# Alternating the order of head-group pairs, so that the last pair's streamed weights serve two steps

## The chip, the cores and the metric

The kernel runs on one core of one Trainium2 chip. The metric is the device time of one execution in microseconds (us), the median of several runs. The profile is one execution taken by the hardware profiler; its span is a little shorter than the device time. Engines are named as in the profile: PE is TensorE's matmul, PEld its weight load, DVE VectorE, ACT ScalarE, POOL GpSimd, SP SyncE, whose queue issues nearly all DMAs here.

## The reference

Four layers are applied to `x` (2048 tokens of 640): A, B, A, B, each with a layer norm before it and a residual around it. The two A layers have the same weights, and so have the two B layers.

```python
def _A_ref(x, mem0, Wq, Wk, Wv, Wo, seg_len):      # 32 heads of 192, 8 memory rows, segments of 32
    mem = mem0
    for s in range(n_seg):                         # 64 segments, one after the other
        h = jnp.concatenate([mem, x[:, s*seg_len:(s+1)*seg_len, :]], axis=1)   # 40 rows
        q, k, v = (jnp.einsum('btd,dhe->bhte', h, W) for W in (Wq, Wk, Wv))
        p = softmax(where(mask, einsum('bhqe,bhke->bhqk', q, k) * scale, -1e9))
        o = jnp.einsum('bhqk,bhke->bhqe', p, v)
        o = jnp.einsum('bhte,hed->btd', o, Wo)
        mem = o[:, :M, :]                          # the memory of the next segment
        outs.append(o[:, M:, :])

def _B_ref(x, w1, w2, w3, w4):                     # a mixer with shifts over tokens, and an MLP
    h = _gelu(_layernorm(x) @ w1)
    x1 = x + shifted(h) @ w2
    return x1 + _gelu(_layernorm(x1) @ w3) @ w4
```

The attention layer is a recurrence: a segment needs the memory rows that the segment before it made. With 40 rows a segment, each weight tile that is loaded into the array serves only 40 columns of moving data. Wq, Wk, Wv and Wo have 7.9 MB each[...].

## The kernel before

**Steps and lanes.** The work is cut into 69 steps (`T_A`). Lane 0 is the first A layer, lane 1 the second A layer, five segments behind (`LAG`). In step `t`, lane 0 handles segment `t` and lane 1 segment `t - 5`, with the same weights. In steps 0 to 4 only lane 0 runs, in steps 64 to 68 only lane 1; the 59 steps between have both. Matmuls of a two-lane step have 80 moving columns, those of a one-lane step `W = max(ONE, 40)`, which is 40. The B layers are computed in chunks of two segments for both lanes at once (`chunk`, `chunk_end`), spread over the attention steps; the last chunk runs alone at the end.

**Inside a step.** The 32 heads are 8 groups of 4, and two groups make a pair. For each of the 4 pairs, `proj_pair` makes k, q and v of both groups (L553: 90 matmuls a group). Then `attend` runs per group: scores (L618), mask and minimum (L629), exponential (L636), row sums and division (L640 to L642), transpose (L651) and its copy (L656), product with v (L665), the copy `oT` out of PSUM (L681), and the output projection (L692: 30 matmuls a group), which adds up in `psy` over the whole step. v itself is made in columns, copied (L583), transposed (L591) and copied into `V` by ACT and DVE in two halves (L602, L600). At the end of a step, L710 copies the new memory rows out of `psy` into `hT`, the moving operand of the next step's projections.

**Weights.** All of Wo stays on the chip, and so does a part of Wq, Wk and Wv: of the five contraction tiles of each kind, `STREAM` says how many are streamed (k 3, q 3, v 2), and `MORE` makes one more tile of k resident for pair 1. The others are loaded in every step, by `load_pair`, into a ring of 8 slots (`RING_A`, tile `wst`, 384 KB a load, L461). A pair has 8 streamed tiles (pair 1 has 7). The B weights stream through a second ring of three slots (`wstB`).

**The order of the work.** Nothing is scheduled by hand. Every operation is given to `Plan.add` with an engine, a cost, a due time and the buffers it reads and writes; `Plan.place` then simulates the engines and places, at each point, the operation that can start first (within 0.12 us on PE, the one with the earliest due time). The program is emitted in this order, and each engine runs its own list in order. PSUM tiles and ring slots are given out as they come free in this simulation. Loads form two queues in order of due time: `wa` for attention weights, `wb` for B weights, both issued by SP. A load is also held back until the simulated DMA is at most `DMA_AHEAD` behind (1 us; `DMA_AHEAD_ONE`, 2 us, where one lane runs). Where this holds a load back, it is made to wait for the last PE operation planned to be over by then. The simulated DMA moves 350 GB/s (`DMA_RATE`), and 385 in the first step (`DMA_START`).

Of the kernel before, what the change touches and what calls it, by code (L numbers as in the profile page):

```python
# [20 lines left out]
LAG = 5  # L21
# [3 lines left out]
MORE = {("k", 1): 1}  # L25
RING_B = 3
STEP = 48.0
Y_POOL = "A"
PSUM_POOLS = {"A": 6, "B": 2}
OT_BUFS = 8  # L30
KT_BUFS = 2
VT_BUFS = 2
HALVES = ()
ONE = 40
WARM = (2, 4, 2, 1, 1, 1, 1, 6, 1, 1, 2, 1, 1)
LAT = 0.12
PE_LAT = 0.3
DMA_RATE = 350.0e3
DMA_ISSUE = 0.37
DMA_FIRST = 0.8  # L40
DMA_LAST = 3.2
B_MARGIN = 0.6
LEAD_A = 0.0
LEAD_B = 0.0
DMA_AHEAD = 1.0
DMA_AHEAD_ONE = 2.0
DMA_START = 385.0e3
NSTEPS = 64
LAST_PACE = 0.55

# [30 lines left out]
class Plan:  # L81
# [48 lines left out]
    def place(self):  # L130
        in_queue = {}
        head = {}
        for q, lst in self.queues.items():
            lst.sort(key=lambda o: (o.due, o.i))
            for k, o in enumerate(lst):
                in_queue[o.i] = (q, k)
            head[q] = 0
        engines = sorted({o.e for o in self.ops})
        cand = {e: [] for e in engines}
        free = dict.fromkeys(engines, 0.0)  # L140
        waiting = {}

        def offer(o):
            if o.i in in_queue:
                q, k = in_queue[o.i]
                if k != head[q]:
                    waiting[o.i] = o
                    return
            cand[o.e].append(o)

        for o in self.ops:
            if o.n == 0:
                offer(o)
        left = len(self.ops)
        srv = 0.0
        out = []

        def est(o, t):
            s = max(t, o.ready)
            need = {}  # L160
            for b in o.slots:
                if b.slot is None:
                    need[b.cls] = need.get(b.cls, 0) + 1
            for c, n in need.items():
                fs = self.free_slots[c]
                if len(fs) < n:
                    return None
                s = max(s, fs[n - 1][0])
            if o.e == "SP":
                s0 = s  # L170
                s = max(s, srv - ahead(o))
                o.paced = s > s0 + 1e-9
            return s

        def ahead(o):
            if o.due < STEP:
                return 1.0e9
            return DMA_AHEAD_ONE if o.due < LAG * STEP or o.due >= NSTEPS * STEP else DMA_AHEAD

        while left:  # L180
            best = None
            for e in engines:
                t = free[e]
                lst = cand[e]
                if not lst:
                    continue
                vals = []
                m = None
                for o in lst:
                    s = est(o, t)  # L190
                    if s is not None:
                        vals.append((s, o))
                        if m is None or s < m:
                            m = s
                if m is None:
                    continue
                if best is not None and m >= best[0]:
                    continue
                lim = m + (0.12 if e == "PE" else 0.05)
                s, o = min((so for so in vals if so[0] <= lim), key=lambda so: (so[1].due, so[1].i))  # L200
                if best is None or s < best[0]:
                    best = (s, o)
            assert best is not None, "no operation can be placed"
            s, o = best
            e = o.e
            for b in o.slots:
                if b.slot is None:
                    b.slot = self.free_slots[b.cls].pop(0)[1]
            o.start = s
            o.end = s + o.d  # L210
            free[e] = o.end
            done = o.end
            if o.dma:
                srv = max(s + DMA_FIRST, srv) + o.dma / (DMA_START if o.due < STEP else DMA_RATE)
                done = srv + DMA_LAST + o.margin
            cand[e].remove(o)
            out.append(o)
            left -= 1
            for b in o.slots:
                b.left -= 1  # L220
                b.free_at = max(b.free_at, done + LAT)
                if b.left == 0:
                    heapq.heappush(self.free_slots[b.cls], (b.free_at, b.slot))
                    self.free_slots[b.cls].sort()
            for x in o.succ:
                if o.dma:
                    at = done
                elif x.e == e:
                    at = o.end
                else:  # L230
                    at = o.end + (PE_LAT if e == "PE" else LAT)
                if at > x.ready:
                    x.ready = at
                x.n -= 1
                if x.n == 0:
                    offer(x)
            if o.i in in_queue:
                q, k = in_queue[o.i]
                head[q] = k + 1
                lst = self.queues[q]  # L240
                if k + 1 < len(lst) and lst[k + 1].i in waiting:
                    x = waiting.pop(lst[k + 1].i)
                    cand[x.e].append(x)
        return out
# [3 lines left out]
def kernel(  # L248
# [17 lines left out]
    P = 128  # L266
    _, S, Dm = A_x.shape
# [8 lines left out]
    NG = H // HG  # L276
    GW = HG * Dh
    GC = GW // P
    GWH = GW // 2
    PW = 2 * GW  # L280
    NPAIR = NG // 2
# [17 lines left out]
    Wo_v = A_Wo.rearrange("h e d -> (h e) d").rearrange("(g c p) d -> p g c d", c=GC, p=P)  # L299
# [150 lines left out]
    def load_pair(kind, pr, due, now):  # L450

        nres = KC - STREAM[kind] + MORE.get((kind, pr), 0)
        cols = slice(PW * pr, PW * (pr + 1))
        rb, rt = res_tile((kind, pr), [P, nres, PW], w_src[kind][:, 0:nres, cols], due)
        slots = []
        for j, kc in enumerate(range(nres, KC)):
            b = Slotted("ra", None)
            b.make = lambda b=b: wring.tile([P, SLOT], bf16, name="wst", tag=f"ra{b.slot}")

            def fn(op, b=b, kc=kc):  # L460
                nc.sync.dma_start(out=T(b)[:, 0:PW], in_=w_src[kind][:, kc, cols])  # L461
            add("SP", DMA_ISSUE, due - now + 0.01 * j, fn, w=(b,), dma=2 * P * PW, queue="wa")
            slots.append(b)

        def view(kc, c0, c1):
            if kc < nres:
                return rt[:, kc, c0:c1]
            return T(slots[kc - nres])[:, c0:c1]
        return (rb, *slots), view
# [35 lines left out]
        return b, view  # L505


    def lanes(t):
        r = []
        if t < NSEG:  # L510
            r.append(0)
        if 0 <= t - LAG < NSEG:
            r.append(1)
        return r
# [4 lines left out]
    def attention_step(t):  # L519
# [9 lines left out]
        base = t * STEP  # L529
# [4 lines left out]
        first_wo = [True]  # L534
        nxt = lanes(t + 1)

        def proj_pair(pr):
            s0 = base + sl * 2 * pr
            for kind, at in (("k", 0.0), ("q", 0.2), ("v", 0.5)):
                wbs, wv = load_pair(kind, pr, s0 + at * 2 * sl, LEAD_A)  # L540
                for j in range(2):
                    g = 2 * pr + j
                    G = t * NG + g
                    due = s0 + (at + 0.1 * j) * 2 * sl
                    pq = ps("A", [P, GC, NS], f32, "ps" + kind)

# [56 lines left out]
                            add("DVE" if hf else "ACT", 0.35 if hf else act_us(GWH), due, fe, r=(pvt,),  # L603
                                w=(B("V", G % VT_BUFS, hf),))

        def attend(g):
            G = t * NG + g
            s0 = base + sl * g
            q, k_, V_ = qT, kT[G % KT_BUFS], Vt[G % VT_BUFS]
            pss = ps("A", [P, HG * NS], f32, "pss")  # L610
            hi = s0 + 0.5 * sl
# [56 lines left out]
            o_ = oT[G % OT_BUFS]  # L668

            oks = [B("oT", G % OT_BUFS, hf) for hf in range(2)]  # L670
            if g in HALVES:
                for hf in range(2):
                    def f7(op, hf=hf):
                        if hf:
                            nc.scalar.copy(out=o_[:, 3:6, off:off + N], in_=T(pso)[:, 3:6, 0:N])
                        else:
                            nc.vector.tensor_copy(out=o_[:, 0:3, off:off + N], in_=T(pso)[:, 0:3, 0:N])
                    add("ACT" if hf else "DVE", (act_us if hf else dve_us)(3 * N), hi - 4, f7, r=(pso,), w=(oks[hf],))
            else:
                def f7(op):  # L680
                    nc.vector.tensor_copy(out=o_[:, :, off:off + N], in_=T(pso)[:, :, 0:N])  # L681
                add("DVE", dve_us(GC * N), hi - 4, f7, r=(pso,), w=oks)
            due = base + STEP - 1 + 0.02 * g if g >= NG - OT_BUFS + 1 else s0 + 2.0 * sl
            wb, wo = res_tile(("o", g), [P, GC, Dm], Wo_v[:, g], base + STEP - 2 + 0.02 * g)
            for hf in range(2):
                def f8(op, hf=hf):
                    o = T(psy)
# [5 lines left out]
                                             rhs=o_[:, cc, 0:W], start=st, stop=True, skip_group_check=True)  # L693
                add("PE", mm_us(W, k=3 * KC), due, f8, r=(wb, oks[hf]), a=(psy,))

        for pr in range(NPAIR):
            proj_pair(pr)
            attend(2 * pr)
            attend(2 * pr + 1)

        due = base + STEP - 5
        hn = hT[(t + 1) % 4]
# [605 lines left out]
```

## Time and profile before

| | |
|---|---|
| time, median of 3 runs (lowest to highest) | 3512.29 us (3511.93 to 3518.08) |
| span of the profiled execution | 3501.2 us |
| granted clock of TensorE, mean | 0.980 |
| DMA in all | 1075.25 MB, 307 GB/s |
| loads of `wst` in the attention layers: q, k, v | 828, 759, 552 |
| loads of `wstB` | 495 of 320 KB, 132 of 160 KB |
| median time from the issue to the landing of a `wst` load | 5.2 to 5.4 us |
| copy of `oT` out of PSUM, two lanes (L681) | 472 of 654 ns |
| the same, one lane | 80 of 404 ns |

The profile comes in several views. The page gives busy time and the span in 40 slices: a digit is tenths of the slice, and PEclk the clock granted to TensorE in tenths of full speed. A second view cuts the span at given times. A third is the chain of waits, followed back from the last instruction. A fourth lists which engine waited for which: the waiting line, what it waited for, then microseconds in total, number of times and the longest. "Issue" there is idle time for which the profile shows no wait. The mean duration of a matmul in the lists contains its passage through the array, which overlaps with the next one; what a stream of matmuls costs is the distance of their starts.

### The profile page before, as it was taken

The numbers are of one execution on the slowest core, as the hardware profiler recorded it, in microseconds if no ns is written. First come the engines' busy times: TensorE is split into PE (matmuls) and PEld (weight loads), VectorE is DVE, ScalarE is ACT, GpSimd is POOL, SyncE is SP. The second block draws the span as 40 slices with busy tenths as digits, with TensorE's granted clock in tenths as the row PEclk, the third lists the DMA queues.
The fourth block names the chain that finished last, engine by engine and source line by source line (L and its number), as shares of the span: only waits on it lengthen the run. The fifth ranks groups of instructions, "written<-read, shape, count | busy, mean of one in ns | idle before, by whom it ended". The sixth has DMA issues, their size and how long they took to land.

```text
span 3501.2 us, 187978 instructions
## 1 busy us (share of the span) xinstructions
PE 3319.2 (95%) x84571; PEld 3225.6 (92%) x84573; DVE 2466.0 (70%) x7360; ACT 1519.5 (43%) x3573; POOL 235.3 (7%) x489
## 2 busy tenths in 40 slices
PE   5889999999999999999999999999999999999887
PEld 5889999999999999999999999999999999999776
DVE  2556777777777777777677777777777777777554
ACT  1334444444444444444444444444444444444333
POOL 1000000000000000000000000000000000000000
PEclk6999999999999999999999999999999999999999
DMA  9999898889888988898889888988898889888996
GB/s 375 319 312 314 301 322 294 297 299 322 306 309 299 323 304 306 305 320 304 294 307 323 302 297 297 323 306 308 308 325 302 293 304 315 301 305 298 316 307 222
DMA packets 497886, 1075.25 MB, mean 307 GB/s; under 512 B 49424, under 2 KB 217055, under 8 KB 497080
## 3 DMA queue, kind: packets, MB, share of 16 engines
q1 hardware_dynamic: 489784, 1050.15, 86.5%
q8 instruction: 661, 10.83, 1.2%
q0 software_dynamic: 7136, 13.00, 1.1%
q14 instruction: 145, 1.19, 0.1%
q10 hardware_dynamic: 160, 0.08, 0.0%
HBM read 1057.79 MB, written 5.24 MB: 304 GB/s over the span
## 4 chain that ended last, share of the span: by engine, by line
PE 90%; DMA 4%; issue 3%; DVE 2%; ACT 1%; SPq 0%; POOL 0%; POOLq 0%; DVEq 0%; ACTq 0%
PE psy L692 16%; PE psq L553 16%; PE psk L553 16%; PE psv L553 15%; PE pvt L591 5%; PE pso L665 4%; PE pss L618 4%; PE psh L1102 3%; PE y L1147 3%; PE pst L651 2%; DMA wst<-in_A_Wk_dram 2%; PE psh L980 1%; PE hs L1039 1%; DMA wst<-in_A_Wq_dram 1%; PE psv L753 1%
## 5 line engine op out<-in xcount | busy, mean ns | idle before, releaser
L553 PEld LDWEIGHTS <-wst 128*128 128x128 bf16 x25668 | 1030.7, 100 | 35.8 <-issue 23.4
L692 PE MATMUL psy<-oT,wo 128*128 128x80 bf16 (+1 forms) x16560 | 689.1, 199 | 34.7 <-issue 20.1
L692 PEld LDWEIGHTS <-wo 128*128 128x128 bf16 x16560 | 625.5, 100 | 44.2 <-issue 32.0
L563 ACT CAST qT<-psq 128x480 bf16<-128x480 f32 (+1 forms) x552 | 292.1, 529 | 630.5 <-PE psq L553 628.9
L553 PE MATMUL psq<-hT,wst 128*128 128x80 bf16 (+1 forms) x9936 | 468.2, 199 | 7.2 <-DMA wst<-in_A_Wq_dram 3.6
L681 DVE CAST oT<-pso 128x480 bf16<-128x480 f32 (+1 forms) x552 | 341.2, 618 | 160.8 <-PE pso L665 155.5
L553 PE MATMUL psv<-hT,wv 128*128 128x80 bf16 (+1 forms) x9936 | 433.9, 199 | 16.4 <-issue 12.9
L553 PE MATMUL psk<-hT,wst 128*128 128x80 bf16 (+1 forms) x9108 | 427.6, 199 | 10.0 <-issue 7.6
L656 ACT COPY PT<-pst 80x320 bf16<-80x320 bf16 (+1 forms) x552 | 221.6, 402 | 437.4 <-PE pst L651 429.8
L553 PEld LDWEIGHTS <-wv 128*128 128x128 bf16 x9936 | 386.1, 99 | 23.4 <-issue 14.7
L602 ACT COPY V<-pvt 80x384 bf16<-80x384 bf16 x552 | 261.5, 474 | 329.8 <-PE pvt L591 301.1
L553 PE MATMUL psk<-hT,wk 128*128 128x80 bf16 (+1 forms) x7452 | 349.2, 199 | 22.8 <-issue 11.5
L629 DVE CUSTOM_DVE_ANT_1 pss<-pss,mask 80x320 f32<-80x320 f32 (+2 forms) x552 | 253.8, 474 | 143.0 <-PE pss L618 136.7
L577 DVE CAST kT<-psk 64x160 bf16<-64x160 f32 (+1 forms) x1104 | 336.6, 305 | 9.8
L636 ACT ACTIVATE Pm<-pss,sm 80x320 bf16<-80x320 f32 (+2 forms) x552 | 279.3, 506 | 136.0 <-DVE sm L629 135.8
L583 ACT CAST vF<-psv 128x480 bf16<-128x480 f32 (+1 forms) x552 | 289.6, 525 | 103.9 <-PE psv L553 97.9
L553 PE MATMUL psv<-hT,wst 128*128 128x80 bf16 (+1 forms) x6624 | 322.6, 199 | 11.6 <-issue 10.5
L553 PE MATMUL psq<-hT,wq 128*128 128x80 bf16 (+1 forms) x6624 | 319.7, 199 | 7.7 <-issue 3.7
L553 PEld LDWEIGHTS <-wk 128*128 128x128 bf16 x7452 | 299.0, 100 | 29.5 <-issue 29.0
L600 DVE COPY V<-pvt 80x384 bf16<-80x384 bf16 x552 | 188.5, 350 | 174.6 <-PE pvt L591 102.4
L571 DVE CAST kT<-psk 128x320 bf16<-128x320 f32 (+1 forms) x552 | 254.5, 461 | 71.5 <-PE psk L553 65.1
L591 PE MATMUL pvt<-ident,vF 128*128 128x128 bf16 x3312 | 282.3, 222 | 10.1 <-issue 7.3
(139 smaller groups left out, 4354.3 us busy)
## 6 DMA issues: line engine op xcount, KB each, us to landing
wst<-in_A_Wq_dram SPq DMA_DIRECT2D x828, 384.0 KB, 5.3
wst<-in_A_Wk_dram SPq DMA_DIRECT2D x759, 384.0 KB, 5.2
wst<-in_A_Wv_dram SPq DMA_DIRECT2D x552, 384.0 KB, 5.4
wstB<-in_B_w_dram SPq DMA_DIRECT2D x495, 320.0 KB, 4.9
wstB<-in_B_w_dram SPq DMA_DIRECT2D x132, 160.0 KB, 4.6
wo<-in_A_Wo_dram SPq DMA_DIRECT2D x8, 960.0 KB, 12.5
wv<-in_A_Wv_dram SPq DMA_DIRECT2D x4, 1152.0 KB, 11.7
wq<-in_A_Wq_dram SPq DMA_DIRECT2D x4, 768.0 KB, 11.7
```

The costliest lines, as they stand in the source:

```text
L553: nc.tensor.matmul(out=o[:, cc, 0:W], lhsT=wv(kc, GW * j + cc * P, GW * j + (cc + 1) * P), rhs=h[:, kc, cw:cw + W], start=(kc == 0 and cc ...
L563: nc.scalar.copy(out=q[:, :, c0:c0 + N], in_=T(pq)[:, :, off:off + N])
L571: nc.vector.tensor_copy(out=k4[:, :, 0::3, c0:c0 + N], in_=p4[:, :, 0::2, off:off + N])
L577: nc.vector.tensor_copy(out=k4[r0:r1, :, jj, c0:c0 + N], in_=p4[r0:r1, :, 1, off:off + N])
L583: nc.scalar.copy(out=vF[:, :, c0:c0 + N], in_=T(pq)[:, :, off:off + N])
L591: nc.tensor.transpose(out=o[0:w_, c * P:(c + 1) * P], in_=vFw[:, c * NS:c * NS + w_], identity=ident[:, :])
L602: nc.scalar.copy(out=dst, in_=src)
L629: nc.vector.tensor_tensor_reduce(out=o, in0=o, in1=maskt.unsqueeze(1).to_broadcast([NR, HG, N]), scale=-scale, scalar=3.0e38, op0=ALU.add, ...
L636: nc.scalar.activation(out=Pb[0:NR, :, c0:c0 + N], in_=o, func=ACT.Exp, bias=sm_[0:NR, 0:1], scale=-1.0)
L656: nc.scalar.copy(out=Pt[:, :, 0:N], in_=T(pst)[0:NS, :, c0:c0 + N])
L681: nc.vector.tensor_copy(out=o_[:, :, off:off + N], in_=T(pso)[:, :, 0:N])
L692: nc.tensor.matmul(out=o[:, m, cw:cw + W], lhsT=wo[:, cc, m * P:(m + 1) * P], rhs=o_[:, cc, 0:W], start=st, stop=True, skip_group_check=True)
```

## The change

The four pairs of head groups are gone through from 0 to 3 in even steps and from 3 to 0 in odd ones. The pair that ends a step then begins the next one, and its streamed tiles can stay in the ring: they are loaded once for two steps. The buffers of k, V and `oT` now go by the position in the step, and the weights by the true number of the group.

With it come three settings. `HALVES` makes the copy `oT` two copies in every group, one of DVE and one of ACT. `ONE` widens the matmuls of one-lane steps from 40 to 56 columns; the additional 16 columns aren't used, and what they are for is to keep TensorE more active. And the plan of the one-lane steps expects 400 GB/s (`RATE_ONE`) and holds loads to 1 us ahead in place of 2.

```diff
+KEEP = True
-HALVES = ()
-ONE = 40
+HALVES = tuple(range(8))
+ONE = 56
-DMA_AHEAD_ONE = 2.0
+DMA_AHEAD_ONE = 1.0
+RATE_ONE = 400.0e3
...
-                srv = max(s + DMA_FIRST, srv) + o.dma / (DMA_START if o.due < STEP else DMA_RATE)
+                srv = max(s + DMA_FIRST, srv) + o.dma / (DMA_START if o.due < STEP else RATE_ONE if alone(o) else DMA_RATE)
...
+    kept = {}
...
-        def proj_pair(pr):
-            s0 = base + sl * 2 * pr
+        def proj_pair(i_, pr):
+            s0 = base + sl * 2 * i_
             for kind, at in (("k", 0.0), ("q", 0.2), ("v", 0.5)):
-                wbs, wv = load_pair(kind, pr, s0 + at * 2 * sl, LEAD_A)
+                if i_ == 0 and t > 0 and KEEP:
+                    wbs, wv = kept[kind]
+                else:
+                    wbs, wv = load_pair(kind, pr, s0 + at * 2 * sl, LEAD_A)
+                if i_ == NPAIR - 1:
+                    kept[kind] = wbs, wv
...
-            if g in HALVES:
+            if p_ in HALVES:
...
-        for pr in range(NPAIR):
-            proj_pair(pr)
-            attend(2 * pr)
-            attend(2 * pr + 1)
+        for i_ in range(NPAIR):
+            pr = NPAIR - 1 - i_ if t % 2 and KEEP else i_
+            proj_pair(i_, pr)
+            attend(2 * i_, 2 * pr)
+            attend(2 * i_ + 1, 2 * pr + 1)
```

In the same way `attend` takes the position `p_` beside the group `g`: due times and buffers go by `p_`, and only the tile of Wo goes by `g`.

More of the change, by code (lines that the diff above doesn't have):

```diff
@@ L177, in ahead, with alone @@
                 return 1.0e9
-            return DMA_AHEAD_ONE if o.due < LAG * STEP or o.due >= NSTEPS * STEP else DMA_AHEAD
+            return DMA_AHEAD_ONE if alone(o) else DMA_AHEAD
+        def alone(o):
+            return o.due < LAG * STEP or o.due >= NSTEPS * STEP
         while left:
@@ L535, in attention_step @@
         nxt = lanes(t + 1)
-        def proj_pair(pr):
-            s0 = base + sl * 2 * pr
+        def proj_pair(i_, pr):
+            s0 = base + sl * 2 * i_
             for kind, at in (("k", 0.0), ("q", 0.2), ("v", 0.5)):
-                wbs, wv = load_pair(kind, pr, s0 + at * 2 * sl, LEAD_A)
+                if i_ == 0 and t > 0 and KEEP:
[4 more added lines that the diff above has]
+                    kept[kind] = wbs, wv
                 for j in range(2):
-                    g = 2 * pr + j
-                    G = t * NG + g
+                    G = t * NG + 2 * i_ + j
                     due = s0 + (at + 0.1 * j) * 2 * sl
@@ L604, in proj_pair, with attend @@
                                 w=(B("V", G % VT_BUFS, hf),))
-        def attend(g):
-            G = t * NG + g
-            s0 = base + sl * g
+        def attend(p_, g):
+            G = t * NG + p_
+            s0 = base + sl * p_
             q, k_, V_ = qT, kT[G % KT_BUFS], Vt[G % VT_BUFS]
@@ L682, in attend @@
                 add("DVE", dve_us(GC * N), hi - 4, f7, r=(pso,), w=oks)
-            due = base + STEP - 1 + 0.02 * g if g >= NG - OT_BUFS + 1 else s0 + 2.0 * sl
-            wb, wo = res_tile(("o", g), [P, GC, Dm], Wo_v[:, g], base + STEP - 2 + 0.02 * g)
+            due = base + STEP - 1 + 0.02 * p_ if p_ >= NG - OT_BUFS + 1 else s0 + 2.0 * sl
+            wb, wo = res_tile(("o", g), [P, GC, Dm], Wo_v[:, g], base + STEP - 2 + 0.02 * p_)
             for hf in range(2):
```

## The prediction

> **What bounds the kernel now.** I read the page first, then busy time by step, then the chain of waits in two short windows, then who waits for whom in the stages with two lanes and with one.
>
> The page: TensorE is busy almost all the time, the weights stream on one queue, and TensorE's clock is below full only near the two ends.
>
> ```profile
> PE 3319.2 (95%) x84571; PEld 3225.6 (92%) x84573; DVE 2466.0 (70%) x7360; ACT 1519.5 (43%) x3573; POOL 235.3 (7%) x489
> ...
> PEclk6999999999999999999999999999999999999999
> DMA  9999898889888988898889888988898889888996
> ...
> q1 hardware_dynamic: 489784, 1050.15, 86.5%
> ...
> q8 instruction: 661, 10.83, 1.2%
> ```
>
> Busy time cut at the 68 `hT` copies of L710, which end the steps (us; then busy time and count by engine, clock, DMA share, GB/s):
>
> ```profile
> 88.10:133.20 45.10, 37.51 (x1152) 35.47 (x1152) 20.41 (x81) 13.81 (x41) 0.00 (x0) 0.88 0.93 321
> ...
> 278.30:3232.40 2954.10, 2887.82 (x72353) 2824.77 (x72350) 2180.42 (x6300) 1342.49 (x3064) 202.06 (x411) 1.00 0.89 307
> ...
> 3280.00:3328.90 48.90, 41.92 (x1206) 39.44 (x1204) 24.89 (x94) 16.84 (x50) 4.53 (x8) 0.87 0.93 312
> ...
> 3427.80:3501.00 73.20, 54.57 (x1308) 45.68 (x1309) 35.47 (x122) 21.60 (x62) 1.86 (x4) 0.92 0.60 204
> ```
>
> The 59 two-lane steps take 2954.1/59 = 50.1 us each. The one-lane steps are hardly shorter (190.2/4 = 47.6 at the start, 195.4/4 = 48.9 at the end), though each matmul has half the columns.
>
> The chain in order of time gives the price of a matmul: 1.72/48 = 35.8 ns with 80 columns, and with 40 columns 0.45/18 = 25 ns at full clock, 2.16/60 = 36 ns where the clock is not granted throughout.
>
> ```profile
> 1002.67 1.72 PE psk L553 x48
> ```
>
> ```profile
> 3428.01 2.16 PE psk L553 x60
> ...
> 3448.29 0.45 PE psv L553 x18
> ```
>
> Who waits for whom on TensorE (us in total, times, longest), first 278 to 3232 us, then 3232 to 3428 us:
>
> ```profile
> PE psy L692 <- issue: 17.2, 28, 1.5
> PE psv L553 <- issue: 12.4, 19, 1.3
> PE psk L553 <- ACT hT L710: 9.1, 29, 0.3
> ...
> PE psq L553 <- DMA wst<-in_A_Wq_dram: 1.2, 2, 0.8
> ```
>
> ```profile
> PE psk L553 <- issue: 7.7, 6, 2.5
> PE pvt L591 <- issue: 6.9, 3, 3.0
> ...
> PE pst L651 <- DVE Pm L642: 2.4, 6, 0.8
> ```
>
> What to see: in neither stage does TensorE wait for weights to speak of. It waits for "issue". I set each such gap beside the packets of queue q8, the instruction fetches of 16 KB: in every one I looked at, a fetch starts 2.2 to 3.1 us and ends about 1.2 to 1.7 us before TensorE resumes. These are fetch stalls. I then took each distance between two matmul starts, less the price of the first (35.8 ns, 25 ns, 56 ns at 128 columns, 136 ns at 320). Two-lane, 96 us of the 2954 are lost so, 68 to fetches; one-lane, 48.5 us of the first four steps and 48.1 of the last four, 20.3 and 24.8 to fetches. The rest is the attention chain, the step boundary and a clock not fully granted.
>
> Does weight traffic make the stalls? I sorted the 565 two-lane fetches by the bytes all queues moved in the 4 us before each. Of 79 that followed under 250 GB/s none stalled. The 486 others (86%) stalled by 0.14 us on average.
>
> **What the Trainium skill says.** "Runtime: NRT & Kernel Launch", section "Instruction fetch mechanics": instructions come in blocks of 16 KiB over a DMA queue of the sequencer's own, a cost "mostly hidden". The trace agrees on size and queue, but 127 of 565 fetches were not hidden. "DMA: Bandwidth & Descriptors", section "Queues, rings and completion order": each DMA engine takes turns between queues packet by packet, so a fetch waits behind weight packets; this fits the 0 of 79. "TensorE: Matmul & The Clock Gate", section "Back-to-back issue gap": N/2.4 + 2.5 ns when warm, never under about 25 ns. The trace has 25 ns at 40 columns and 35.8 at 80. For 56 columns, which it does not show, I take that formula: 25.8 ns.
>
> **The change, part by part.**
>
> *Kept weights, alternating direction.* The 2139 loads of `wst` are 31 a step. Of these, 8 (3 k, 3 q, 2 v, none covered by the extra resident tile of pair 1) belong to the pair that now stays, from step 1 on: 68 x 8 = 544 loads of 393,216 B, 213.9 MB, go. Per two-lane step traffic falls from 307 GB/s x 50.1 us = 15.4 MB to 12.2 MB, by 20%. No matmul goes: TensorE's work in a two-lane step stays (2954 - 96)/59 = 48.4 us.
>
> The cost: at a step's end all 8 slots of the ring hold the kept pair, and nothing streams until the next step's first k projections are through. What queues behind a load that waits for a slot on SyncE is the other loads, those of the mixer's weights too. Does the stream then fit? 23 loads at about 350 GB/s take 1.12 us each; with the mixer's 2.8 MB a step among them, (9.04 + 2.8)/350 = 33.8 us. It starts at about 2.2 us (60 matmuls of 35.8 ns), and the last tile lands some 4 us after it was read: 40 us into the step. What must follow, the last v projections, two attention chains, output projections and the `hT` copy, is about 7 us. 47 is below 50.1: it fits, with 3 us to spare. I take the wait for weights as 0, with up to 1.5 us a step as the other end.
>
> *Two-lane gain.* The share of fetches that meet a loaded queue should fall with the bytes, 86% to 68%: 68 us become 54, so 14 us. The known waits for weights, 6 us in all, lose a quarter, 1.5 us.
>
> *Output halves (HALVES).* The copy `oT` out of `pso` (654 ns on DVE) becomes a DVE half (404 ns, the row with 240 columns) and an ACT half (358 ns, the row of `qT` with 240). They are likely to run one after the other: V's two halves do, DVE waiting for ACT 67.5 us in 97 cases. The first half of the output projection can still start 250 ns sooner; its 15 matmuls (0.54 us) cover the second copy. ACT gains 8 x 0.36 = 2.9 us a step and is at 45%, hidden by TensorE. I count 1 us in all.
>
> *56 columns.* 960 matmuls a step (720 projections, 240 output) at 25.8 instead of 25 ns: +0.8 us a step. The denser array should keep the clock granted (0.87 to 0.98 now), which returns about as much. If it stays ungranted for 18% of the time, at N/1.2 = 46.7 instead of 33 ns, it costs 2.4 us a step; if always granted it gains. I take 0.
>
> *One-lane gain.* The work proper is 35.4 us (first four) and 36.8 (last four). Now the steps move 321 x 45.1 = 14.5 MB and more at a DMA share of 0.93, and the order written out is that of a stream-limited plan: attention waits are left bare. With 12 MB, a plan that expects 400 GB/s and a shorter run ahead (1 us instead of 2), I expect fetch stalls to fall by 30%, from 5.1 and 6.2 to 3.6 and 4.4 us a step, and the rest, 7.0 and 5.8, to about 3. That makes 42.0 and 44.2 us, or 22 + 19 = 41 us. The last attention step, inside 3427.8:3501, gives some 4. The first (to 88 us) is bound by loading all resident weights, where nothing is removed: 0.
>
> Sum: 14 + 1.5 + 1 + 41 + 4 = 61.5 us; 3512.3 - 61.5 = 3451.
>
> **Rivals.** (A) The forecast, 3451: chance 0.60. (B) The stalls don't follow the bytes, since loads run as dense as before while they run, and one-lane steps gain half: 22 us, 3490: 0.18. For it: above 250 GB/s the mean stall hardly grows with the rate. Against: 0 of 79 below. (C) Fetches are freed more than in proportion, 40 us two-lane, and one-lane steps approach their 37 us: 65 us; 3407: 0.12. For it: waits of the attention chain are in the written order, which is new. Against: the stream alone needs nearly 40 us of a one-lane step. (D) The locked ring becomes the bound: 1.5 us a step for 59 steps is 88 us more, less 45 from the one-lane steps: 3555, slower: 0.10. For it: the margin of 3 us rests on a steady 350 GB/s. Against: TensorE has mixer and output work to put in between.
>
> **How the numbers follow.** A, B and C are faster by over 7 us (0.2%): 0.90 less 0.02 for B ending near zero. The range takes A's unknowns and reaches towards B and C: two-lane gain 0 to 40, one-lane gain 20 to 70; 3398 to 3493.
>
> **What would show it.** The loads of `wst` fall to 1595, and queue q1 to about 836 MB. Two-lane steps come to about 49.8 us, one-lane steps to 42 to 44 with PEclk nearer 1. "Issue" waits fall by a fifth two-lane, by a third one-lane; waits for `wst` stay under 10 us. I am wrong if projections of the second pair wait for `wst` in each step, if issue waits keep their size, or if matmuls with 56 columns run at over 30 ns.

## The result, and the profile after

The changed kernel takes 3461.14 us (median of 4 runs, 3459.17 to 3471.07), the kernel before, run beside it, 3515.18 us (3511.93 to 3524.74). The ratio is 0.9848, with a 95% interval of 0.982 to 0.9875: faster by 54 us. The forecast was 3451, with 3398 to 3493 as its range.

The page of the changed kernel, the same lines as before:

```profile
PE 3308.8 (95%) x84571; PEld 3218.5 (93%) x84573; DVE 2338.5 (67%) x7360; ACT 1700.1 (49%) x4125; POOL 235.6 (7%) x489
...
PEclk8999999999999999999999999999999999999999
DMA  9777777667766876677668666876787668766775
...
q1 hardware_dynamic: 411448, 836.21, 70.5%
q8 instruction: 661, 10.83, 1.2%
...
wst<-in_A_Wq_dram SPq DMA_DIRECT2D x624, 384.0 KB, 5.2
wst<-in_A_Wk_dram SPq DMA_DIRECT2D x555, 384.0 KB, 5.0
wst<-in_A_Wv_dram SPq DMA_DIRECT2D x416, 384.0 KB, 5.3
```

624 + 555 + 416 are the 1595 loads foretold, and queue q1 carries 836 MB in place of 1050. The DMA share falls from nines and eights to sixes and sevens. TensorE has the same number of matmuls and hardly less busy time.

Busy time by stage, cut at the `hT` copies, now in L722 (us; busy time and count of PE, PEld, DVE, ACT, POOL; clock, DMA share, GB/s). The first two rows are one-lane steps, the third holds the 59 steps with two lanes, the last the final attention step and the last chunk:

```profile
89.10:133.80 44.70, 37.71 (x1152) 36.55 (x1152) 19.18 (x81) 15.60 (x49) 0.00 (x0) 0.89 0.60 206
...
228.90:275.20 46.30, 40.80 (x1262) 39.10 (x1262) 31.46 (x119) 21.28 (x63) 2.42 (x6) 1.00 0.76 255
275.20:3203.70 2928.50, 2882.80 (x72328) 2821.76 (x72328) 2061.79 (x6300) 1504.21 (x3535) 202.47 (x411) 1.00 0.73 246
...
3394.80:3469.00 74.20, 52.00 (x1308) 43.35 (x1309) 34.29 (x122) 23.17 (x70) 1.86 (x4) 0.99 0.61 201
```

The two-lane stage is 25.6 us shorter (2954.1 before). The one-lane steps are hardly shorter, though nearly a quarter of their traffic and about half of what the clock lacked are gone: the first step with a single lane after the start took 45.1 us and takes 44.7, at a DMA share of 0.60 in place of 0.93.

Who waits for whom on TensorE, 278 to 3232 us, then 3232 to 3428 us:

```profile
PE psv L564 <- issue: 11.2, 16, 1.4
PE psk L564 <- ACT hT L722: 9.4, 30, 0.3
PE psy L703 <- issue: 4.9, 5, 1.4
PE psq L564 <- DVE V L611: 4.5, 29, 0.2
PE psq L564 <- issue: 4.4, 8, 1.2
PE psq L564 <- DMA wst<-in_A_Wq_dram: 3.0, 6, 0.9
```

```profile
PE psy L703 <- issue: 6.7, 5, 2.2
PE psq L564 <- issue: 5.3, 5, 1.3
PE psv L564 <- issue: 4.2, 4, 1.5
PE psk L564 <- issue: 4.1, 5, 1.4
PE psv L765 <- issue: 2.8, 1, 2.8
```

In the first, the largest issue wait of before (`psy`, 17.2 us) is 4.9, and the largest wait for weights has grown from 1.2 to 3.0 us. In the second, issue is all that leads the list; `pst` waiting for `Pm`, third among the lines shown of before, is gone. The windows are the same stretches of time as before. In the changed kernel, which is ahead by then, the last one-lane steps are 3203.7 to 3394.8 us, and there too the first six waits of the list are for issue.

I sorted the gaps between matmul starts as in the prediction. A further count confirms that the gaps sorted as fetch stalls are that. TensorE's 169,144 matmuls and weight loads make 256 for each of the 661 fetches. Counted in blocks of 256, all 170 fetch stalls in the trace of before begin at the same instruction of their block, and so do 108 of 109 in the changed kernel. That is what is to be expected if TensorE runs dry where the instructions fetched so far end, and it speaks against any wait for data. A fetch starts 2.4 us before TensorE resumes, in the middle case of both traces.

The next table has all stages, in us, from the profiled executions of six kernels; the last four columns belong to experiments told below (`after_again` is the changed kernel once more). One-lane is the sum of the eight full steps.

| | before | after | after_again | no_keep | keep_only | light |
|---|---|---|---|---|---|---|
| up to the end of the first step | 88.1 | 89.1 | 88.7 | 89.0 | 88.5 | 88.9 |
| one-lane steps | 385.6 | 377.2 | 372.9 | 391.3 | 384.4 | 324.7 |
| two-lane steps | 2954.1 | 2928.5 | 2924.4 | 2968.0 | 2928.1 | 2885.4 |
| final step and last chunk | 73.4 | 74.6 | 74.1 | 72.7 | 75.3 | 68.3 |
| fetch stalls, two-lane | 68.1 | 32.2 | 28.5 | 69.2 | 37.5 | 0.0 |
| fetch stalls, one-lane | 45.1 | 50.4 | 50.9 | 57.2 | 46.3 | 6.6 |
| waits for other engines, two-lane | 26.5 | 35.4 | 37.8 | 37.9 | 29.8 | 35.1 |
| waits for other engines, one-lane | 35.4 | 18.7 | 19.0 | 21.2 | 34.8 | 20.1 |
| waits for weights, two-lane | 6.3 | 9.6 | 7.2 | 7.8 | 7.5 | 0.0 |

The profiled execution of before (3502.9 us) is 12 us under the median of its kernel and that of the changed kernel (3471.1) 10 us over its own. So the stages add up to a difference of 32 us, or 41 with the second trace, and not to 54. A stage of one execution differs from that of another of the same kernel by some us, as the columns `after` and `after_again` show. The three kinds of two-lane wait of before add up to 101 us in the table, where the prediction counted 96 lost in all.

### The profile page after: what moved, and what is told of

It is laid out like the page before. It is cut to its first block, busy times and chain, and to the rows that moved or that the text cites. A ratio compares the mean times of both kernels' runs of the same rounds, so it can differ in the third digit from the quotient of the medians.

```text
span 3469.4 us, 187478 instructions
## 1 busy us (share of the span) xinstructions
PE 3308.8 (95%) x84571; PEld 3218.5 (93%) x84573; DVE 2338.5 (67%) x7360; ACT 1700.1 (49%) x4125; POOL 235.6 (7%) x489
## 4 chain that ended last, share of the span: by engine, by line
PE 89%; DMA 5%; issue 3%; DVE 1%; ACT 1%; SPq 1%; POOL 0%; POOLq 0%; ACTq 0%; DVEq 0%
PE psy L703 16%; PE psv L564 16%; PE psq L564 16%; PE psk L564 15%; PE pvt L602 5%; PE pss L629 4%; PE pso L676 4%; PE psh L1114 3%; PE y L1159 3%; PE pst L662 2%; DMA wst<-in_A_Wq_dram 2%; DMA wst<-in_A_Wv_dram 2%; PE psh L992 1%; PE hs L1051 1%; PE psv L765 1%
## 5 line engine op out<-in xcount | busy, mean ns | idle before, releaser
L564 PE MATMUL psq<-hT,wst 128*128 128x80 bf16 (+1 forms) x9936 | 455.7, 200 | 19.6 <-issue 11.7
L688 DVE CAST oT<-pso 128x240 bf16<-128x240 f32 (+1 forms) x552 | 213.0, 386 | 301.1 <-ACT oT L686 288.2
L564 PEld LDWEIGHTS <-wv 128*128 128x128 bf16 x9936 | 388.0, 100 | 20.1 <-issue 13.7
L686 ACT CAST oT<-pso 128x240 bf16<-128x240 f32 (+1 forms) x552 | 190.1, 344 | 276.1 <-PE pso L676 210.5
L564 PEld LDWEIGHTS <-wk 128*128 128x128 bf16 x7452 | 298.0, 99 | 20.6 <-issue 20.1
L651 DVE TENSOR_REDUCE sm<-Pm 80x4 f32<-80x320 bf16 (+2 forms) x552 | 249.4, 452 | 72.2 <-ACT Pm L647 67.2
```

The source lines that it names most:

```text
L564: nc.tensor.matmul(out=o[:, cc, 0:W], lhsT=wv(kc, GW * j + cc * P, GW * j + (cc + 1) * P), rhs=h[:, kc, cw:cw + W], start=(kc == 0 and cc ...
L651: nc.vector.tensor_reduce(out=sm_[0:NR, 2:2 + HG], in_=Pb[0:NR, :, c0:c0 + N], axis=AX.X, op=ALU.add)
```

## The experiments

All are edits of the changed kernel. Times are medians with the range of the runs; ratios are to the kernel before, run beside them.

**The two halves of the change.** First the kept pair alone, then all but the kept pair.

```diff
-HALVES = tuple(range(8))
-ONE = 56
-DMA_AHEAD_ONE = 1.0
-RATE_ONE = 400.0e3
+HALVES = ()
+ONE = 40
+DMA_AHEAD_ONE = 2.0
+RATE_ONE = 350.0e3
```

> Only the kept pair with its alternating order; copies in one piece, 40 columns, 2 us ahead and 350 GB/s in one-lane steps, as in the kernel before. Theory T (the gain is two-lane fetch stalls that the missing bytes free; the settings are worth little): two-lane steps about 49.7 us, two-lane fetch stalls 30 to 40 us, time 3455 to 3475. Rival R1 (the copies in halves and the new plan carry the gain): two-lane stalls back near 60 us and the time within 10 us of before, over 3500.

Measured: 3479.73 us (3473.26 to 3484.09), ratio 0.9891 (0.9871 to 0.9911). Two-lane steps take 49.6 us each with 37.5 us of fetch stalls in all. That is as T says, though the time is 5 us over its range. The one-lane steps are as before, 384.4 us with 46.3 us of stalls.

```diff
-KEEP = True
+KEEP = False
```

> The changed kernel without the kept pair: all 31 loads a step, always in order 0 to 3, the other settings as changed. T: two-lane fetch stalls 60 to 70 us again, two-lane steps about 50.1 us, time 3500 to 3520. R1: stays near 3465 with stalls near 35 us.

Measured: 3517.91 us (3508.2 to 3522.8), ratio 0.9991 (0.9975 to 1.0007): no change at all. Stalls are back at 69.2 us two-lane and rise to 57.2 one-lane, as T says. So the kept pair carries the gain, 39.7 us by itself (before took 3519.42 us beside it). The other settings show no gain without it. With it they seem to add 0.4%: the eight runs of the changed kernel (3459.17 to 3471.07 us) and the four of the kept pair alone don't overlap, though they didn't run beside each other, and the intervals of 0.9848 and 0.9891 touch. No run alternates the order and still loads all 31 tiles, so the order by itself isn't separated from the missing loads.

**Is it the traffic that makes the issue gaps?** Every streamed load of attention weights after the first step brings a quarter of its columns, so three quarters of these weights are left out. All instructions and waits stay as they are.

```diff
+        part = PW if due < STEP else PW // 4
...
-                nc.sync.dma_start(out=T(b)[:, 0:PW], in_=w_src[kind][:, kc, cols])
+                nc.sync.dma_start(out=T(b)[:, 0:part], in_=w_src[kind][:, kc, PW * pr:PW * pr + part])
...
-            return T(slots[kc - nres])[:, c0:c1]
+            return T(slots[kc - nres])[:, c0 % part:c0 % part + c1 - c0]
```

> The changed kernel with every streamed load of the attention weights after the first step cut to a quarter of its columns, and the matmuls reading that quarter in place of the rest; so three quarters of the streamed weights are left out. Order, waits and number of instructions are the same. T: fetches meet an empty queue, issue waits of TensorE fall under 10 us in all, one-lane steps fall to 39 to 41 us, two-lane steps to 49.1 to 49.3, time 3375 to 3400. Rival R3 (the attention chain or the written order holds the one-lane steps, and the issue gaps only stand in for it): one-lane steps stay over 45 us, time over 3430.

Measured: 3368.06 us (3366.3 to 3369.43), ratio 0.9574 (0.9559 to 0.9588). Busy time by stage in that kernel (first one-lane steps, two-lane, last one-lane steps):

```profile
88.90:249.80 160.90, 152.13 (x4867) 147.40 (x4867) 106.07 (x412) 75.86 (x232) 7.63 (x17) 0.99 0.40 112
249.80:3135.20 2885.40, 2869.14 (x72328) 2817.49 (x72328) 2061.14 (x6300) 1501.48 (x3536) 202.08 (x411) 1.00 0.39 111
3135.20:3299.00 163.80, 155.17 (x4906) 149.97 (x4906) 111.46 (x425) 77.91 (x235) 13.91 (x29) 0.99 0.43 125
```

One-lane steps take 324.7/8 = 40.6 us and two-lane steps 48.9, and TensorE's waits for issue are gone from the head of the list, 278 to 3232 us:

```profile
PE psk L565 <- ACT hT L723: 9.9, 32, 0.3
PE psq L565 <- DVE V L612: 4.5, 29, 0.2
PE psn L766 <- DVE h2u L758: 1.1, 1, 1.1
```

T is borne out and R3 falls: with the same written order and the same attention chain, 93 us go with the traffic (3461.1 - 3368.1), about half of them in the one-lane steps (324.7 us against 377.2 and 372.9), somewhat more than T had said. By the table, 76 us of fetch stalls go in the steps (32.2 two-lane, 43.8 one-lane), and the 9.6 us of two-lane waits for weights with them. Not one of 565 two-lane fetches stalls.

**The columns.**

```diff
-ONE = 56
+ONE = 40
```

> The changed kernel with 40 columns in one-lane steps. T: one-lane steps last as long as an instruction fetch every 4.9 us, so the columns matter little: one-lane steps 46 to 48 us, total within 6 us of the changed kernel, granted clock there falling from 0.96 to about 0.92. Rival R2 (the wider matmuls hold the clock and so carry the one-lane gain): one-lane steps 1 to 2 us longer each, total 10 to 18 us more.

Measured: 3468.88 us (3465.99 to 3473.89), ratio 0.9862 (0.9847 to 0.9877). The one-lane steps take 375.8 us, inside what the two traces of the changed kernel show, with a granted clock of 0.91 and 0.94 (0.96 in the changed kernel). T holds as to the steps. The total is 7 to 8 us above the changed kernel's, more than T's 6, in intervals that overlap, so a small gain from the columns isn't excluded. R2's full 10 us isn't seen.

**The copy in two halves.**

```diff
-HALVES = tuple(range(8))
+HALVES = ()
```

> The changed kernel with the copy of oT in one piece on DVE. The prediction's step: worth 1 us. Rival (the two copies, one after the other on two engines, disturb the attention chain or help it): over 8 us either way, seen in the two-lane dependency waits, 35 us now.

Measured: 3462.67 us (3462.46 to 3477.72), ratio 0.9843 (0.9812 to 0.9874): worth nothing that can be seen. Waits for other engines in two-lane steps fall from 35.4 to 28.5 us, but fetch stalls are 42.0 instead of 32.2, and the stage takes 2930.1 us, about the same. The one-lane steps take 365.6 us in this trace, 7 to 12 less than in the changed kernel, which the total doesn't show. A reason why the copies bring nothing stands in the list of groups of the changed kernel (busy us, mean ns of one, then idle time before it and what ended it):

```profile
L688 DVE CAST oT<-pso 128x240 bf16<-128x240 f32 (+1 forms) x552 | 213.0, 386 | 301.1 <-ACT oT L686 288.2 <-PE pso L676 9.5
```

DVE waits for ACT's half: the two run one after the other.

**The plan of the one-lane steps.** First as it was, then with a lower rate than before.

```diff
-DMA_AHEAD_ONE = 1.0
-RATE_ONE = 400.0e3
+DMA_AHEAD_ONE = 2.0
+RATE_ONE = 350.0e3
```

> The changed kernel with the plan of the one-lane steps as it was: 350 GB/s expected and loads held to 2 us ahead. T' (loads that run dense delay the fetches whatever is planned; one-lane stalls don't follow the mean traffic): one-lane fetch stalls stay at 45 to 55 us for the eight steps, total within 8 us of the changed kernel. Rival (expecting 400 GB/s overfills the queue and made the stalls rise): stalls fall by 10 us or more and the total with them.

Measured: 3474.51 us (3459.57 to 3477.33), ratio 0.9869 (0.984 to 0.9897). One-lane stalls are 41.0 us, below what T' gave and nearly what the rival gave; but waits for other engines rise from 18.7 to 33.9 us, and the steps take 374.9 us, the same. Neither theory had that trade. The total is 13 us above the changed kernel's, more than T' allows, but the profiled execution was the fastest of the four (3459.57 us, the others 3473.62 and more), so its trace doesn't show where these 13 us lie.

```diff
-RATE_ONE = 400.0e3
+RATE_ONE = 300.0e3
```

> The changed kernel with 300 GB/s in place of 400 expected in one-lane steps, so that loads are issued further apart. T': fetches then find gaps between loads, one-lane stalls fall from 50 to 25 to 35 us, one-lane steps to 44 to 45.5 us, total 3440 to 3450. Rival (the loads are bound by slots coming free and not by the plan's pace): stalls stay near 50 us and the total within 6 us.

Measured: 3479.86 us (3477.21 to 3487.8), ratio 0.9885 (0.9858 to 0.9912). The stalls fall to 26.4 us, inside T', but the steps get longer, 391.7 us. Who waits for whom on TensorE there, 3205 to 3405 us:

```profile
PE pst L662 <- DVE Pm L653: 6.3, 6, 1.2
PE psq L564 <- issue: 4.7, 4, 1.9
...
PE pso L676 <- ACT V L613: 2.9, 3, 1.0
```

Waits for other engines are 57.1 us in place of 18.7. So T' holds for the stalls and fails for the time, and the rival falls. I take it that a plan that expects a slow stream writes an order in which the attention chain is left bare; no run has the old order with the slower pace.

**The same in two-lane steps.**

```diff
-DMA_RATE = 350.0e3
+DMA_RATE = 300.0e3
```

> The changed kernel with 300 GB/s in place of 350 expected in two-lane steps. T': two-lane stalls fall from 32 to 10 to 20 us, waits for weights stay under 20 us, total 3440 to 3452. Rival (the slack left by the locked ring is too small for slower loads): waits for weights rise above 40 us and the total above 3480.

Measured: 3524.53 us (3517.97 to 3538.07), ratio 0.9999 (0.9982 to 1.0017). Fetch stalls nearly vanish (3.8 us) and waits for weights are 2.0 us, so the rival falls; but waits for other engines go from 35.4 to 130.2 us, and the whole gain is lost. The list of waits, 278 to 3232 us:

```profile
PE psy L703 <- DVE oT L688: 25.8, 29, 0.9
PE psy L703 <- ACT oT L686: 13.6, 30, 0.6
PE pvt L602 <- ACT vF L594: 12.0, 28, 0.4
```

**Smaller loads with the order kept.** To have gaps between the loads and the dense order too, each load was cut in two.

```diff
...
-            add("SP", DMA_ISSUE, due - now + 0.01 * j, fn, w=(b,), dma=2 * P * PW, queue="wa")
+            b2 = Buf()
+            for u in range(2):
...
+                add("SP", DMA_ISSUE, due - now + 0.01 * j + 0.001 * u, fn, w=(b2 if u else b,), dma=P * PW, queue="wa")
...
```

With it went the changed kernel once more, without an edit, and the half loads with a shorter run ahead:

```diff
-DMA_AHEAD = 1.0
-DMA_AHEAD_ONE = 1.0
+DMA_AHEAD = 0.8
+DMA_AHEAD_ONE = 0.8
```

> The changed kernel itself once more, beside the two that follow. Both theories: 3458 to 3475.

> The changed kernel with each streamed load of the attention weights issued as two loads of half the columns, each held to the plan's pace by itself. The bytes, the expected rate and the work of TensorE are the same. Theory Q (a fetch waits for what is queued ahead of it when it is asked for; a load adds about 1.1 us of work to that queue, half a load 0.6): fetch stalls fall by a quarter to a half, from about 82 us (two-lane 32, the eight one-lane steps 50) to 45 to 60, total 3435 to 3450. Rival (only bytes over some microseconds count, not the size of a load): stalls stay within 8 us of the changed kernel and so does the total.

> The same with loads held to 0.8 us ahead of the planned stream in place of 1. Q: 5 to 10 us less again in stalls. Rival: no difference, or more waits for weights than it saves.

Measured: the changed kernel 3461.96 us (3459.23 to 3463.72), ratio 0.9836 (0.9799 to 0.9873); half loads 3508.88 (3493.99 to 3521.7), ratio 0.9973 (0.9957 to 0.9989); with 0.8 us ahead 3510.63 (3494.22 to 3522.3), ratio 0.9978 (0.9964 to 0.9992). Fetch stalls fall further than Q said, to 7.8 us two-lane and 17.4 one-lane. TensorE now also waits for weights, which gives the fetches time, so the stalls alone don't show that the size of a load counts. The start of the fetches does. Counted from the instruction 300 before the one at which stalls begin, a fetch that follows over 250 GB/s starts after 2.72 us two-lane and 3.04 one-lane, where it was 3.08 and 4.06 in the changed kernel. The shorter run ahead makes no difference (6.6 and 16.5 us of stalls). But the weights now come late, as the waits of the half loads show, 278 to 3232 us:

```profile
PE psq L566 <- DMA wst<-in_A_Wq_dram: 27.5, 34, 1.5
PE psv L566 <- DMA wst<-in_A_Wv_dram: 9.1, 16, 1.8
PE psk L566 <- ACT hT L724: 9.1, 29, 0.3
PE y L1161 <- DMA wstB<-in_B_w_dram: 8.4, 13, 1.6
```

In all, two-lane waits for weights are 77 us in place of 7 to 10. Two causes are possible. In the trace the issues on SP follow each other by 0.51 us in the middle case, 192 KB each, so the number of issues could hold the stream back where it has to hurry; but that is still 385 GB/s, more than the 350 planned. And the packets are half as long, 1.5 KB that take 65 ns in the middle case where 3 KB took 121, which is 7% more time for the same bytes. No run separates the two.

**Half loads in one-lane steps alone**, since these gained (363.2 us in place of 372.9).

```diff
...
+            nu = 2 if STEP <= due < LAG * STEP or due >= NSTEPS * STEP else 1
+            for u in range(nu):
...
```

> The changed kernel with the loads of the attention weights in two halves in the one-lane steps alone; two-lane steps keep whole loads. Theory Q with the limit found: one-lane fetch stalls near 17 us instead of 50, weight waits there 20 to 25 us, two-lane steps as in the changed kernel, total 8 to 12 us below it, 3448 to 3456. Rival (two-lane steps feel it too, through the queue of SP): two-lane steps over 49.9 us and no gain.

Measured: 3460.5 us (3447.86 to 3465.97), ratio 0.9854 (0.9827 to 0.988). One-lane stalls are 24.1 us in place of 50, waits for weights there 28.9, and the steps take 370.7 us. The two-lane steps stay at 49.6 us, so the rival's reason falls. But what is won in stalls is given back in waits for weights, and the total is that of the changed kernel, not the 8 to 12 us below it that Q gave. No version tried beats it beyond doubt.

## Why the prediction was right, and where it was not

**Direction and total: right.** The forecast was 61.5 us, measured were 54. In the two-lane steps the cause was the one given: less traffic, fewer fetch stalls. But the two main terms were off in opposite directions. The traces show 26 and 30 us two-lane where 16.5 were forecast (14, 1.5 and 1), and 8 and 13 us one-lane where 41 were. That the total came so near is luck in part; the stages of the traces account for 32 to 41 us of the 54.

**The locked ring costs nothing: right.** Two-lane waits for weights are 9.6 and 7.2 us, before 6.3. The forecast had 1.5 us less. It took the slack of 3 us a step as enough, and it is. With 300 GB/s planned, too, weights come in time (2.0 us of waits), though the steps are longer then, 50.6 us.

**Two-lane stalls: mechanism right, size too small.** The forecast scaled only the share of fetches that meet a loaded queue, 86% to 68%, and left the stall of each at 0.14 us; 14 us in all. In the changed kernel 367 of 566 fetches, 65%, follow over 250 GB/s: that term was right. But each of these now loses 0.09 us, not 0.14, so that stalls fall by 36 to 40 us. With the same settings and no kept pair each loses 0.14 again, with the kept pair alone 0.10, so it is the kept pair. The traces show a part of how. Counted from the instruction 300 before the one at which stalls begin, as for the half loads, a loaded fetch starts after 3.28 us before and after 3.08 and 3.11 us in the two traces after, and TensorE reaches the place where it runs dry after 6.1 to 6.2 us in all three. With the 2.4 us from the start of a fetch to TensorE's resuming, most fetches come just in time, only the late ones cost, and 0.2 us on all of them takes away much of that cost. Why a loaded fetch starts sooner, no run shows.

**One-lane steps: the term that failed.** The forecast was 41 us, of which fetch stalls were to fall by 30%, from 45 to 32 us. They did not fall: 45.1 before, 50.4 and 50.9 after. One of the prediction's own signs of being wrong, issue waits that keep their size, came true here. The steps gained 8.4 us by the first trace and 12.7 by the second. Of the 28 to 32 us that are missing, 19 are the stalls. The rest of the losses, over the work proper of 35.4 and 36.8 us a step, was to fall from 51 us to 24 and fell to 38 and 33; the waits for other engines in it fell from 35.4 to 18.7.

The settings and the kept pair have different shares in this. The kept pair alone leaves stalls and other waits as they were (46.3 and 34.8 us). The settings alone lower the other waits to 21.2 and raise the stalls to 57.2. With both, `old_plan` and `pace_one` show the same exchange: where the chain waits less, fetches wait more.

The share of fetches that meet a loaded queue did fall, from 71 of 76 to 46 of 76; but each of those now stalls by 0.97 us where it was 0.60. The traces show two parts of that. Counted in the same way, a loaded fetch starts later, after 4.06 and 4.24 us where it was 3.65 (4.00 with the settings alone, 3.85 with the kept pair alone). And TensorE gets to the place where it runs dry sooner, after 5.68 and 5.80 us where it was 5.88. The first part is the larger in this count; a count from an earlier instruction brings the two nearer to each other, and at which instruction a fetch is asked for isn't seen. So what TensorE wins elsewhere can come back as a stall, but that is not all of it. `light` shows the other side: without the loads the steps fall to 40.6 us.

In the prediction's words, the error is in taking the stalls as a cost beside the other waits that falls with the bytes. The two were in part in exchange, and a loaded fetch didn't get cheaper here. What the runs show to lower the stalls is to load at a slower planned pace (26.4 us with 300 GB/s planned) or in smaller loads (17.4 us), neither of which made the kernel faster, and not fewer bytes at the same density.

**56 columns: right within what can be seen.** The price of 25.8 ns that I took from "TensorE: Matmul & The Clock Gate" in the Trainium skill ("Back-to-back issue gap") is what the chain of the changed kernel shows in a one-lane step, 0.78/30 = 26.0 ns:

```profile
3305.08 0.78 PE psv L564 x30
```

That section gives its formula for an isolated matmul and a longer gap, about 81 ns at 128 columns, for a stream of pairs of weight load and matmul. The runs here are such streams, and they show 55 to 56 ns at 128 columns, so the formula is what holds. Where the granted clock was 0.5, starts were 33 ns apart with 40 columns before and 46 to 47 ns with 56 after, as the prediction had them. The clock rises from 0.91 and 0.93 to 0.96 and more, and the sum was put at 0; `one40` leaves room for some us.

**Output halves: right**, 1 us forecast and none seen, and the two copies do run one after the other.

**First step: right**, 88.1 and 89.1 us. **Final step: wrong by 5 us**, the 4 us expected there are not in the traces (73.4 before, 74.6 and 74.1 after); fetch stalls there rose from 5.1 us to 9.9 and 9.3.

Of the rivals, B had the small one-lane gain, with a reason that holds for the one-lane stage only; C had the two-lane fetches freed more than in proportion (36 to 40 us of stalls, 26 to 30 us of time); D, the ring as the new bound, did not come.

## What to carry to other kernels

When a profile shows idle time of TensorE with no wait behind it, set the gaps beside the instruction queue's packets, and cut the traffic with the order unchanged to see their worth: here 93 us, more than the whole change brought. Then count where in the instruction stream the gaps begin; here all but one of the fetch stalls of the two kernels begin at the same instruction of their block of 256. Two waits that stand in each other's shadow can't be added up as separate gains: between `old_plan` and the changed kernel the chain waits 15 us less, the fetches 9 more, and the steps last as long as they did. And a planner's assumed rate is both a pace and an order: lowering it freed the fetches and brought the waits for other engines back.

## What the runs showed of the hardware that was not expected

- Instruction fetches of TensorE, 661 blocks of 16 KB and 1.2% of the DMA engines' time, cost up to 113 us of the kernel before (68.1 + 45.1), where "Runtime: NRT & Kernel Launch" in the Trainium skill ("Instruction fetch mechanics") calls the cost "mostly hidden". That agrees with 438 of the 565 two-lane fetches and not with the other 127. Halving the size of the loads at the same bytes took the stalls of the changed kernel from 79 to 83 us down to 25, in part because TensorE then waited for weights instead.
- Fetch stalls are sensitive to small shifts. With a quarter fewer loaded fetches, and these starting 0.2 us sooner on average, two-lane stalls more than halved (68.1 us to 32.2 and 28.5).
- Two half loads are not one whole load: the issues came 0.51 us apart in the middle case, packets of half the size took 7% more time for the same bytes, and two-lane waits for weights rose by about 70 us.
